# Batch 0's transposed keys are kept in HBM scratch by the first run and loaded back, instead of transposed again

## The chip, the cores and the metric

The kernel runs on one core of a Trainium2 chip. The metric is device time in microseconds (us), the median of three runs. The engines are PE (TensorE, matrix multiply and transpose), DVE (VectorE), ACT (ScalarE), POOL (GpSimd) and SP (SyncE, which here only issues DMAs). Each engine works through its own instructions strictly in the order in which they were written; they meet through semaphores.

## What is computed

Causal attention with a gated linear memory, and behind it a dense mixture of four experts. Cut to what matters:

```python
# q, k, v: (B, H, S, D) = (4, 8, 576, 64)
scores = q @ k.T / sqrt(D), causal mask
a = exp(scores - max); a /= a.sum(-1) + 1e-9
local = a @ v
q_p = phi(q)                                  # elu(q) + 1
mem_out = (q_p @ M_prev) / (q_p @ z_prev + 1e-6)
x = g * mem_out + (1 - g) * local             # g = sigmoid(beta), per head
x = x.transpose(0, 2, 1, 3).reshape(2304, 512)
for e in range(4):                            # w1: (4, 512, 1024), w2: (4, 1024, 512)
    out += p[:, e:e+1] * (relu(x @ w1[e]) @ w2[e])
```

## The kernel before

**Attention.** Heads are taken in pairs, so a tile of 128 partitions holds two heads of 64. The 576 positions are five chunks: four of 128 and a tail of 64. A run is a batch with a set of query chunks: `CA` is chunks 0 and 1, `CB` is chunks 2, 3 and 4. The eight runs go batch 0 to 3 with `CA`, then batch 0 to 3 with `CB`. A task is a run and a head pair.

The very first run, batch 0 with `CA`, is `first_run`. Its order is written out by hand as a string of words, `ORDER`; each word calls the function `f_...` of that name (`ck2` is `f_ck(2)`). It works in plain float32. For head pair `a`, `f_tr` transposes queries and keys on PE, and `f_ck` (a DVE copy) or `f_ka` (an ACT copy) puts the transposed keys of chunks 0 and 1 into the tile `kT[a]`, 128 x 256. The words `d0` to `d10` are matmuls on a tile of zeros whose results nobody reads.

The tiles `qT[a]` and `kT[a]` borrow the buffers of later tiles. For an even `a` they use the tags "ex" and "rl", with one buffer each; for an odd `a` they use two buffers of the tag "qp". So `kT[0]` and `kT[2]` are the same memory, one after the other.

The 28 other tasks are `tasks[0..27]`. Tasks 0 to 11 are `CA` of batches 1 to 3, tasks 12 to 15 are `CB` of batch 0, and tasks 16 to 27 are `CB` of batches 1 to 3. A task loads q, k and v (`t_load`), transposes its key chunks from `t.k0` on into a PSUM tile (`t_trk`), and splits them into a high part rounded to float32r (`k_hi`, two ACT instructions, one per head half) and the rest (`k_lo`, two DVE instructions). `t_cpk` duplicates the high parts over the partition halves by DMA. Tasks 0 to 11 also store the split keys in HBM scratch (`t_keep`), and tasks 16 to 27 take them back (`t_take`), so that they transpose chunks 2 and 3 alone (`t.k0 = 2`). Tasks 12 to 15 transpose all four (`t.k0 = 0`).

**Experts.** The matmuls take each float32 product as three float32r products (high by high, high by low, low by high): `mm1` (L958) and `mm2` (L990) for the phases beside the attention, `pass_parts` (L1189, L1267) for the phases behind it. Weights come by `w_dma` and are split by `w_prep` on ACT and POOL.

**What sets the order.** Attention events carry a slot and a weight (`ev`); the main loop puts attention steps between matmul parts whenever the weight done so far falls behind a target. The weights of `t_trk` count the chunks that it transposes. SP issues nearly all DMAs, each on one of eight completion lanes in turn, and an issue waits until the DMA eight issues before it has landed.

Of the kernel before, what the change touches and what calls it, by code (L numbers as in the profile page):

```python
# [8 lines left out]
F32 = mybir.dt.float32  # L9
# [40 lines left out]
def tile_attention_moe(  # L50
# [13 lines left out]
    nc = tc.nc  # L64
    P = 128
# [9 lines left out]
    CA, CB = (0, 1), (2, 3, 4)  # L75
    NCH = 5
# [25 lines left out]
    GW = 2 * P  # L102
# [8 lines left out]
    dram = ctx.enter_context(tc.tile_pool(name="dram", bufs=1, space=bass.MemoryType.DRAM))  # L111
# [6 lines left out]
    def f(ap):  # L118
        return ap.bitcast(F32)
# [19 lines left out]
    for i in range(2):  # L139
        o, d = i * 12 * P, {}  # L140
# [92 lines left out]
    def batch_load(r):  # L233
        b = r[0]
        zb = att.tile([P, H, D], F32, tag="zb", name=f"zb{b}_{r[1][0]}", bufs=2)
        nc.sync.dma_start(out=zb, in_=z_prev[b : b + 1].partition_broadcast(P)[:, 0])
        bdat[r] = [zb, None, None]

    def batch_load_m(r):
        b = r[0]  # L240
        mr = att.tile([P, H, D], F32, tag="mr", name=f"mr{b}_{r[1][0]}", bufs=1)
        for i in range(2):
            nc.sync.dma_start(
                out=mr[i * D : (i + 1) * D], in_=M_prev[b].rearrange("h d e -> d h e")
            )
        bdat[r][1] = mr
# [16 lines left out]
    for b, cs in RUNS[1:]:  # L263
        for a in range(NPAIR):
            t = Task()
            t.b, t.cs, t.a, t.i, t.s0 = b, cs, a, len(tasks), pos
            t.run = (b, cs)
            t.nk = cs[-1] + 1
            t.k0 = 2 if cs == CB and b else 0
            t.q0 = cs[0] * P  # L270
            t.nq = min((cs[-1] + 1) * P, S) - t.q0
            t.nat, t.qk = NAT[t.i % 2], QK[t.i % 2]
            pos += 4 if cs == CA else 5
            tasks.append(t)
        run_end[t.run] = pos - 1 + 3
# [5 lines left out]

    kept = {}

    def t_load(t, names="qkv"):
        for n, src, c0 in (("q", q, t.cs[0]), ("k", k, t.k0), ("v", v, 0)):
            if n not in names:
                continue
            nfull = min(t.nk, NCH - 1) - c0
            for j in range(2):
                s_ = src[t.b, 2 * t.a + j]  # L290
                nc.sync.dma_start(
                    out=t.nat[n][:, 0:nfull, j],
                    in_=s_[c0 * P : (c0 + nfull) * P].rearrange("(c p) d -> p c d", p=P),
                )
            if t.nk == NCH:
                for r in {"q": (D,), "k": (0,), "v": (0, D)}[n]:
                    to = t.nat["q"][:, 2] if n == "k" else t.nat[n][:, nfull]
                    nc.sync.dma_start(
                        out=to[r : r + S - 4 * P],
                        in_=src[t.b, 2 * t.a : 2 * t.a + 2, 4 * P : S].rearrange(  # L300
                            "h p d -> p h d"
                        ),
                    )
# [53 lines left out]
    def tr(dst, src, n):  # L357
        nc.tensor.transpose(dst, src, ident[0:n, 0:n])  # L358

    def to_tile(name):  # L360
        return ps.tile([P, 512], F32, tag="to", name=name, bufs=2)
# [19 lines left out]
    def k_hi(pt, qk, c0, n):  # L381
        o = slice(c0, c0 + n)
        for x, k_ in ((A, qk["kha"]), (Bh, qk["khb"])):
            nc.scalar.activation(k_[x, o], pt[x, 0:n], AF.Copy)

    def k_lo(pt, qk, c0, n, joint=False):
        o = slice(c0, c0 + n)
        for h, (x, k_) in enumerate(((A, qk["kha"]), (Bh, qk["khb"]))):
            l_ = qk["qz"][x, h * GW : h * GW + n] if joint else qk["kl"][x, o]
            nc.vector.tensor_tensor(l_, pt[x, 0:n], f(k_[x, o]), ALU.subtract)  # L390

    def dup_k(qk, c0, n, eng):
        o = slice(c0, c0 + n)
        for x, y, k_ in ((A, Bh, qk["kha"]), (Bh, A, qk["khb"])):
            eng.dma_start(out=f(k_[y, o]), in_=f(k_[x, o]))

    def copier(t):
        return nc.sync if t.i else nc.scalar

    def flat(ap):  # L400
        return ap.rearrange("p j d -> p (j d)")
# [24 lines left out]
    def t_cpq(t):  # L426
        dup_k(t.qk, 4 * P, D, copier(t))

    def t_trk(t):
        pt = to_tile(f"tk{t.i}")  # L430
        m = min(t.nk, NCH - 1) - t.k0
        for c in range(m):
            tr(pt[:, c * P : (c + 1) * P], flat(t.nat["k"][:, c]), P)
        k_hi(pt, t.qk, t.k0 * P, m * P)
        k_lo(pt, t.qk, t.k0 * P, m * P, t.joint)
        if t.joint:
            t_cpk(t)

    def t_cpk(t):
        dup_k(t.qk, t.k0 * P, (min(t.nk, NCH - 1) - t.k0) * P, copier(t))  # L440

    def t_keep(t):
        kh, kl = (
# [358 lines left out]
    def ev(slot, prio, fn, cost=0.0, vec=0.0):  # L802
        wt = PR["wvec"] + PR["wpe"] * cost + vec
        events.setdefault(slot, []).append((prio, len(events.get(slot, [])), fn, wt))

    def dv(n):
        return 150.0 + n / 0.96

    seen = set()
    for t in tasks:  # L810
        s0 = t.s0
        ld = -9 + t.i if t.i < 2 else s0 - 7
        PQ = PR
        n = len(t.cs)
        if t.run not in seen:
            seen.add(t.run)
            ev(s0 - 9, 9 if t.i else 6, lambda r=t.run: batch_load(r))
            ev(s0 - (5 if t.i else 8), 9, lambda r=t.run: batch_load_m(r))
            ev(s0 + (2 if t.joint else 3), 9 if t.joint else 0.1, lambda r=t.run: batch_prep(r))
            if t.cs == CB and t.b == 0:  # L820
                for i in range(2):
                    ev(s0 - 12, 9, lambda i=i: zeros(i))
        if t.joint:
            ev(ld, 6.3, lambda t=t: t_load(t))
        else:
            ev(s0 - 8, 8, lambda t=t: t_load(t, "qk"))
            ev(s0 - 6, 8, lambda t=t: t_load(t, "v"))
        if t.i:
            p1, p2 = (PQ["phi1"], PQ["phi2"]) if t.i > 1 else ((-4, 6.75), (-4, 7))
            ev(s0 + p1[0], p1[1], lambda t=t: t_phi1(t))  # L830
            ev(s0 + p2[0], p2[1], lambda t=t: t_phi2(t), 0.0, dv(n * P))
        ev(
            s0 + (PQ["phi3"][0] if t.i > 1 else (0, -3)[t.i]),
            PQ["phi3"][1] if t.i > 1 else (6.6, 19)[t.i],
            lambda t=t: t_phi3(t),
            0.0,
            600.0 if t.joint else 750.0,
        )
        ev(s0 - 3 if t.i else s0, 20 if t.i else 6.7, lambda t=t: t_phi4(t))
        if t.i == 0:  # L840
            ev(s0 - 1, 5, lambda t=t: t_trq(t), 109.0 * n, 2 * dv(n * P))
        else:
            ev(s0 + PQ["trq"][0], PQ["trq"][1], lambda t=t: t_trq(t), 109.0 * n, 2 * dv(n * P))
            ev(
                s0 + PQ["trk"][0],
                PQ["trk"][1],
                lambda t=t: t_trk(t),
                109.0 * (t.nk - t.k0),
                2 * dv((4 - t.k0) * P),
            )  # L850
        if not t.joint:
            ev(s0 + PQ["trq"][0] + 1, 0.5, lambda t=t: t_cpq(t))
            ev(s0 + PQ["trk"][0], 2.4, lambda t=t: t_cpk(t))
        if t.joint:
            ev(s0 + 1, 9, lambda t=t: t_keep(t))
        elif t.k0:
            ev(s0 + PQ["trk"][0], 2.3, lambda t=t: t_take(t))
        ev(s0, PQ["v"], lambda t=t: t_v(t))
        ev(
            s0 + PQ["trqp"][0 if t.joint else 2],  # L860
            PQ["trqp"][1],
            lambda t=t: t_trqp(t),
            109.0 * n,
            2 * dv(t.nq),
        )
    for i, s in slots.items():
        w = wid(s.c)
        t = s.t
# [444 lines left out]
    def first_run():  # L1313
        b = FIRST[0]
# [8 lines left out]
        qT, kT, tf, pf, st, ptp, pw, tpf, of = ({} for _ in range(9))  # L1323
# [190 lines left out]
        def f_ldv(c):  # L1514
            for j in range(2):
# [2 lines left out]
                    in_=v[b, j:H:2, c * P : (c + 1) * P].rearrange("a p d -> p a d"),  # L1518
                )

        def f_tq(a):
            tpf[a] = to_tile(f"tpf{a}")
            for c in range(2):
                tr(tpf[a][:, c * P : (c + 1) * P], qp[c][:, a], P)
# [74 lines left out]
        d1 tr0 eb0 d2 cq0 ka0 sc0 sc1 mk00 mk01 tr1 ex00 mk10 d7 ex01 mk11 rc0 d9 ex10  # L1599
        ex11 ck1 rc1 cq1 r1 tr2 np00 ck2 e1 r0 nd11 p1 d0 np01 pt0 np10 sc3 mk30 z1 pa0  # L1600
        mk31 d5 e0 ex31 p0 sc2 mk20 ex30 mk21 tr3 d8 rc3 cq2 rr1 z0 ka3 d10 cq3 ex20 rn1
        ldv1 d6 nm30 nm31 pt1 rr0 ldv0 pa1 sc4 rn0 go9 pt3 mk40 ex21 pa3 mk41 m1 ex40
        rc2 ex41 sc5 nd21 m0 mk50 sc7 np20 tq2 tq0 mk51 eq2 ev0 w0 rc4 pt2 ex50 tq3 sc6
        eq3 mk70 mk71 tq1 ex51 rc5 pa2 ou0 np40 eq1 np41 ex71 pt4 nm51 nd50 mk60 xh0 pt5
        ex60 xl0 ex70 pa5 mk61 pv4 rc7 w1 ou1 ex61 xh1 w2 rc6 xl1 np70 nd71 ou2 nd60
# [25 lines left out]
        for word in ORDER.split():  # L1631
            name = word.rstrip("0123456789")
# [9 lines left out]
        out=mask[:, 4 * P :],  # L1642
        in_=mask[:, 4 * P :],
# [19 lines left out]
    def zeros(i):  # L1663

        nc.gpsimd.memset(f(QK[i]["qb"][:, 2 * P : 3 * P - D]), 0.0)
# [104 lines left out]
```

## Time and profile before

| what | us |
|---|---|
| median of three runs | 977.03 (976.89 to 977.69) |
| the profiled execution: its own time | 976.75 |
| the profiled execution: its span | 974.9 |
| PE busy in the span | 968.4 (99%) |
| DVE, ACT, POOL busy | 664.8, 569.3, 592.3 |

The profile is of one execution. "Busy" is time in which an engine has an instruction in flight. A busy PE need not do useful work: the matmuls on zeros count as well. The chain of waits follows the work that ended last back to its causes, and names at each moment the engine or the DMA that the end depended on. A timeline lists one engine's instructions in order of time; SPq and ACTq are the parts of these engines that issue DMAs.

### The profile page before, as it was taken

The numbers are of one execution on the slowest core, as the hardware profiler recorded it, in microseconds if no ns is written. First come the engines' busy times: TensorE is split into PE (matmuls) and PEld (weight loads), VectorE is DVE, ScalarE is ACT, GpSimd is POOL, SyncE is SP. The second block draws the span as 40 slices with busy tenths as digits, with TensorE's granted clock in tenths as the row PEclk, the third lists the DMA queues.
The fourth block names the chain that finished last, engine by engine and source line by source line (L and its number), as shares of the span: only waits on it lengthen the run. The fifth ranks groups of instructions, "written<-read, shape, count | busy, mean of one in ns | idle before, by whom it ended". The sixth has DMA issues, their size and how long they took to land.

```text
span 974.9 us, 16235 instructions
## 1 busy us (share of the span) xinstructions
PE 968.4 (99%) x5022; PEld 815.7 (84%) x5022; DVE 664.8 (68%) x1787; ACT 569.3 (58%) x1389; POOL 592.3 (61%) x621
## 2 busy tenths in 40 slices
PE   8999999999999999999999999999999999999998
PEld 6889888888888899888888888888888888888887
DVE  6888888988888888888888888834334253342533
ACT  7888866776666788766666675643424233252430
POOL 7999856765665667865568355677255472544620
PEclk9999999999999999999999999999999999999999
DMA  7777565654444267644545332241111111111102
GB/s 176 193 185 220 155 168 147 168 152 110 115 125 119 77 172 197 179 134 107 130 115 139 87 93 66 66 130 55 55 44 55 54 55 53 46 54 46 53 1 87
DMA packets 188263, 106.77 MB, mean 110 GB/s; under 512 B 91664, under 2 KB 168080, under 8 KB 188176
## 3 DMA queue, kind: packets, MB, share of 16 engines
q1 hardware_dynamic: 187600, 105.60, 39.9%
q8 instruction: 40, 0.66, 0.3%
q14 instruction: 47, 0.39, 0.1%
q10 hardware_dynamic: 544, 0.13, 0.1%
q0 software_dynamic: 32, 0.00, 0.0%
HBM read 93.23 MB, written 7.86 MB: 104 GB/s over the span
## 4 chain that ended last, share of the span: by engine, by line
PE 94%; DVE 2%; POOL 1%; DMA 1%; issue 0%; SPq 0%; ACT 0%; DVEq 0%; ACTq 0%
PE y L990 22%; PE h L958 22%; PE y L1267 18%; PE x L1189 9%; PE z L1189 5%; PE pt L358 4%; PE sp L668 4%; PE o L787 4%; PE y L1189 2%; PE o L609 1%; PE tp L358 1%; PE tq L358 1%; PE tk L358 1%; PE sp L523 1%; PE o L781 0%
## 5 line engine op out<-in xcount | busy, mean ns | idle before, releaser
L227 POOL TENSOR_TENSOR w2l<-stg,w2h 128x512 fp32r<-128x512 f32 x128 | 167.4, 1316 | 147.6 <-ACT w2h L224 143.2
L958 PE MATMUL h<-xh,w 128*128 128x512 f32 (+1 forms) x768 | 243.7, 368 | 0.0
L227 POOL TENSOR_TENSOR w<-stg,w 128x512 fp32r<-128x512 f32 x96 | 124.9, 1308 | 139.6 <-ACT w L224 132.5
L958 PEld LDWEIGHTS h<-xh,w 128*128 128x128 f32 x768 | 138.8, 189 | 17.4 <-issue 0.2
L958 PE MATMUL h<-xl,w 128*128 128x512 f32 (+1 forms) x384 | 136.4, 355 | 0.0
L990 PE MATMUL y<-w2h,hh 128*128 128x512 f32 x320 | 134.4, 420 | 0.0
L990 PE MATMUL y<-w2h,hl 128*128 128x512 f32 x320 | 126.2, 394 | 0.2 <-DVE hl L968 0.2
L990 PE MATMUL y<-w2l,hh 128*128 128x512 f32 x320 | 125.8, 393 | 0.3 <-POOL w2l L227 0.3
L1284 DVE SCALAR_TENSOR_TENSOR acc<-y,pn,acc 128x512 f32<-128x512 f32 (+1 forms) x57 | 41.6, 740 | 82.2 <-PE y L1267 82.2
L725 ACT ACTIVATE pt<-pt 128x384 fp32r<-128x384 f32 (+3 forms) x128 | 50.3, 420 | 64.2 <-PE pt L358 63.2
L958 PEld LDWEIGHTS h<-xl,w 128*128 128x128 f32 x384 | 72.8, 190 | 6.1
L990 PEld LDWEIGHTS y<-w2h,hl 128*128 128x128 f32 x320 | 60.1, 188 | 14.4 <-DVE hl L968 1.0
L990 PEld LDWEIGHTS y<-w2l,hh 128*128 128x128 f32 x320 | 60.5, 189 | 7.9 <-POOL w2l L227 1.1
L990 PEld LDWEIGHTS y<-w2h,hh 128*128 128x128 f32 x320 | 60.3, 188 | 7.8
L967 ACT ACTIVATE hh<-h 128x512 fp32r<-128x512 f32 (+1 forms) x96 | 50.4, 525 | 27.4 <-PE h L958 25.7
L727 DVE TENSOR_TENSOR pt<-pt,pt 128x384 fp32r<-128x384 f32 (+3 forms) x128 | 57.4, 468 | 10.7 <-ACT pt L725 9.4
L968 DVE SCALAR_TENSOR_TENSOR hl<-h,hh 128x512 fp32r<-128x512 f32 (+1 forms) x96 | 57.5, 599 | 8.8 <-ACT hh L967 7.7
L358 PE MATMUL pt<-ident,s 128*128 128x128 f32 (+1 forms) x376 | 60.8, 272 | 0.2
L1213 DVE TENSOR_TENSOR cp_a<-y,cp_a 128x512 f32<-128x512 f32 x16 | 11.1, 692 | 71.4 <-PE y L1189 71.4
L358 PEld LDWEIGHTS pt<-ident,s 128*128 128x128 f32 (+1 forms) x376 | 47.0, 139 | 14.2 <-ACT s L721 0.5
L224 ACT ACTIVATE w<-stg 128x512 fp32r<-128x512 f32 x92 | 57.1, 625 | 0.7
L1006 DVE SCALAR_TENSOR_TENSOR acc<-y,pn,acc 128x512 f32<-128x512 f32 x70 | 52.1, 744 | 6.4 <-PE y L990 5.7
(287 smaller groups left out, 2508.8 us busy)
## 6 DMA issues: line engine op xcount, KB each, us to landing
stg<-in_moe_w_dram SPq DMA_DIRECT2D x256, 256.0 KB, 3.0
natall<-in_v_dram SPq DMA_DIRECT2D x32, 128.0 KB, 3.2
natall<-in_q_dram SPq DMA_DIRECT2D x60, 64.0 KB, 3.0
out_dram<-acc SPq DMA_DIRECT2D x15, 256.0 KB, 2.1
natall<-in_k_dram SPq DMA_DIRECT2D x50, 64.0 KB, 2.5
zb<-in_z_prev_dram SPq DMA_DIRECT2D x7, 256.0 KB, 4.5
mr<-in_M_prev_dram SPq DMA_DIRECT2D x14, 128.0 KB, 3.3
natall<-in_v_dram SPq DMA_DIRECT2D x24, 64.0 KB, 2.2
```

Source lines behind the costliest of these rows:

```text
L224: nc.scalar.activation(hi, t, AF.Copy)
L227: nc.gpsimd.tensor_tensor(lo, t, f(hi), ALU.subtract)
L358: nc.tensor.transpose(dst, src, ident[0:n, 0:n])
L725: nc.scalar.activation(dh, src, AF.Copy)
L727: nc.vector.tensor_tensor(dl, src, f(dh), ALU.subtract)
L958: nc.tensor.matmul(pt[0][:, cols], lhsT=w_[:, c], rhs=x_[:, c, cols], start=(c == 0 and z == 0), stop=(c == NKD - 1 and z == 2),)
L967: nc.scalar.activation(h_, pt[0][:, cols], AF.Relu)
L968: nc.vector.scalar_tensor_tensor(l_, pt[0][:, cols], 0.0, f(h_), ALU.max, ALU.subtract)
L990: nc.tensor.matmul(pt[0], lhsT=h_[fc][:, tk], rhs=w_, start=(fc == 0 and z == 0), stop=(fc == HF - 1 and z == 2),)
L1006: nc.vector.scalar_tensor_tensor(acc[g, tt], pt[0], pe, acc[g, tt], ALU.mult, ALU.add)
L1189: nc.tensor.matmul(k_, lhsT=w_[:, c], rhs=x_[:, c], start=new and n == 0, stop=n == 5, skip_group_check=True,)
L1267: nc.tensor.matmul(y0, lhsT=a[:, tk], rhs=w_[:, x0:x1], start=(fc == 0 and z == 0), stop=(fc == HF - 1 and z == 2),)
```

## The change

`first_run` gets a new word `kp`: `kp0` to `kp3` each issue one DMA from SP that stores `kT[a]` in HBM scratch (`kf`). The first three stand just ahead of the loads of v (`ldv1`), the fourth after `go9`. Tasks 12 to 15 now have `k0 = 2`. They load chunks 2 and 3 naturally and the stored keys of chunks 0 and 1, already transposed, into the free half of their key tile (`raw_k`); they transpose two chunks instead of four, and split the loaded part in four further instructions (two of ACT, two of DVE) that read it from SBUF.

```diff
-            t.k0 = 2 if cs == CB and b else 0
+            t.k0 = 2 if cs == CB else 0
...
+    def raw_k(t):
+        return t.nat["k"][:, 2:4].rearrange("p c j d -> p (c j d)")
...
+            if n == "k" and t.nk == NCH and not t.b:
+                nc.sync.dma_start(out=raw_k(t), in_=kept[t.a])
...
         k_hi(pt, t.qk, t.k0 * P, m * P)
         k_lo(pt, t.qk, t.k0 * P, m * P, t.joint)
+        if t.cs == CB and not t.b:
+            k_hi(raw_k(t), t.qk, 0, GW)
+            k_lo(raw_k(t), t.qk, 0, GW)
...
     def t_cpk(t):
-        dup_k(t.qk, t.k0 * P, (min(t.nk, NCH - 1) - t.k0) * P, copier(t))
+        c0 = t.k0 if t.b else 0
+        dup_k(t.qk, c0 * P, (min(t.nk, NCH - 1) - c0) * P, copier(t))
...
-        elif t.k0:
+        elif t.b:
             ev(s0 + PQ["trk"][0], 2.3, lambda t=t: t_take(t))
...
+        def f_kp(a):
+            kept[a] = dram.tile([P, GW], F32, tag=f"kf{a}", name=f"kf{a}")
+            nc.sync.dma_start(out=kept[a], in_=kT[a])
...
         mk31 d5 e0 ex31 p0 sc2 mk20 ex30 mk21 tr3 d8 rc3 cq2 rr1 z0 ka3 d10 cq3 ex20 rn1
-        ldv1 d6 nm30 nm31 pt1 rr0 ldv0 pa1 sc4 rn0 go9 pt3 mk40 ex21 pa3 mk41 m1 ex40
+        kp0 kp1 kp2 ldv1 d6 nm30 nm31 pt1 rr0 ldv0 pa1 sc4 rn0 go9 kp3 pt3 mk40 ex21 pa3 mk41 m1 ex40
```

Both programs, as built, show where the new instructions stand. First SP in the first run, before. `pn` are expert probabilities, `xr` here holds batch 0's v, and a name such as DMAHW5 is a completion lane.

```order
L1625 DMA xr_100<-in_M_prev_dram 64x4x64 [waits DMAHW2_49]
L925 DMA pn_76<-in_moe_domain_probs_dram 128x4x4 [waits DMAHW3_49]
L925 DMA pn_76<-in_moe_domain_probs_dram 128x4x4 [waits DMAHW4_49]
L1516 DMA xr_100<-in_v_dram 128x4x64 [waits DMAHW5_49,DVE_49]
L1516 DMA xr_100<-in_v_dram 128x4x64 [waits DMAHW6_49]
```

The same place now; `kf0` is the scratch, `tw0_1` is `kT[0]`, `tw1_1` is `kT[1]` and `tw2_1` is `kT[2]`.

```order
L1638 DMA xr_100<-in_M_prev_dram 64x4x64 [waits DMAHW2_49]
L934 DMA pn_76<-in_moe_domain_probs_dram 128x4x4 [waits DMAHW3_49]
L934 DMA pn_76<-in_moe_domain_probs_dram 128x4x4 [waits DMAHW4_49]
L1532 DMA kf0_320<-tw0_1_191 128x256 [waits DMAHW5_49,Activation_49]
L1532 DMA kf1_322<-tw1_1_220 128x256 [waits DMAHW6_49,DVE_49]
L1532 DMA kf2_324<-tw2_1_251 128x256 [waits DMAHW7_49,DVE_49]
L1525 DMA xr_100<-in_v_dram 128x4x64 [waits DMAHW0_49,DVE_49]
```

Three stores stand between the loads of `pn` and of v, and the first of them is the third DMA on lane 5.

Next DVE, around the word `ck2`, which copies the keys of head pair 2 (`tg2`, PSUM) into `kT[2]`. Before:

```order
L1422 RECIPROCAL stf1_223<-stf1_223 128x2 [waits DVE_49]
L1356 COPY tw2_1_251<-tg2_245 128x256 [waits PE_49]
L1438 TENSOR_SCALAR sf1_222,dump_78<-sf1_222,stf1_223 128x256 [waits DVE_49]
L1492 SCALAR_TENSOR_TENSOR xr_100<-natall_79,ep1_254 128x4x128 [waits DMAHW3_49,DMAHW6_49,DMAHW2_49,Activation_49]
L1388 ISA sf3_271,stf3_272<-pf3_0_267,mask_70 128x256 [waits PE_49]
```

Now:

```order
L1431 RECIPROCAL stf1_223<-stf1_223 128x2 [waits DVE_49]
L1365 COPY tw2_1_251<-tg2_245 128x256 [waits DMAHW5_49,PE_49]
L1447 TENSOR_SCALAR sf1_222,dump_78<-sf1_222,stf1_223 128x256 [waits DVE_49]
L1501 SCALAR_TENSOR_TENSOR xr_100<-natall_79,ep1_254 128x4x128 [waits DMAHW3_49,DMAHW6_49,DMAHW2_49,Activation_49]
L1397 ISA sf3_271,stf3_272<-pf3_0_267,mask_70 128x256 [waits PE_49]
```

Nothing moved, but the copy into `kT[2]` has a new wait, on lane 5. In the built program it asks for the lane's third landing, which is that of `kf0`.

Last PE, at the key transposes of task 13 (`tk`); `h` and `y` are expert matmuls. Before:

```order
L958 MATMUL h_3_3060<-xl,w_111 128x512
L958 MATMUL h_3_3060<-xh,w_111 128x512
L358 MATMUL tk_3090<-ident,natall 128x128 x4
L958 MATMUL h_3_3060<-xh,w_111 128x512
L958 MATMUL h_3_3060<-xl,w_111 128x512
```

Now:

```order
L967 MATMUL h_3_3066<-xl,w_111 128x512
L967 MATMUL h_3_3066<-xh,w_111 128x512
L363 MATMUL tk_3107<-ident,natall 128x128 x2
L999 MATMUL y_1_0_3118<-w2h_112,hh_103 128x512
L999 MATMUL y_1_0_3118<-w2l_113,hh_103 128x512
```

Four transposes became two, and the step stands three matmuls later: the smaller weights in `ev` shift the attention steps by a few matmuls against the expert work, here and all through the phases beside the attention.

## Rows read from the trace of the kernel before

**Rows 1.** Page, busy time of each engine, and the granted clock in slices.

```profile
PE 968.4 (99%) x5022; PEld 815.7 (84%) x5022; DVE 664.8 (68%) x1787; ACT 569.3 (58%) x1389; POOL 592.3 (61%) x621
...
PEclk9999999999999999999999999999999999999999
```

**Rows 2.** Stretches: length, busy us of PE, PEld, DVE, ACT, POOL; clock, DMA.

```profile
0.00:25.00 25.00, 22.53 (x139) 15.84 (x140) 17.65 (x86) 18.68 (x61) 17.77 (x34) 1.00 0.77 176
...
50.00:75.00 25.00, 25.00 (x166) 22.30 (x167) 21.13 (x69) 19.82 (x55) 23.04 (x22) 1.00 0.77 197
...
175.00:200.00 25.00, 25.00 (x138) 21.06 (x137) 23.15 (x74) 18.84 (x55) 19.72 (x22) 1.00 0.69 180
```

**Rows 3.** Chain of waits, first 62 us: start, length, what (xcount merged).

```profile
5.40 4.32 DMA natall<-in_k_dram
...
9.76 0.33 PE tg L358
...
13.86 0.70 DVE rp L1501
...
17.56 0.60 POOL w L226
...
30.49 3.42 DMA stg<-in_moe_w_dram
...
48.57 1.29 POOL w2l L227
...
49.90 0.73 PE y L990 x2
...
57.61 0.22 PE tk L358 x2
```

**Rows 4.** Timeline of SP's DMA issues: start, length, line, target, xcount.

```profile
11.56 1.15 SPq L925 DMA_DIRECT2D pn<-in_moe_domain_probs_dram  x2
14.58 2.02 SPq L1516 DMA_DIRECT2D xr<-in_v_dram  x4
...
25.23 0.98 SPq L291 DMA_DIRECT2D natall<-in_v_dram  x2
26.85 1.39 SPq L243 DMA_DIRECT2D mr<-in_M_prev_dram  x2
```

**Rows 5.** Timeline of DVE at the copy into kT[2]; brackets: idle before, releaser.

```profile
10.13 0.43 DVE L1356 COPY tw<-tg 128x256 f32<-128x256 f32 x1 [0.93 <-PE tg L358]
10.47 0.47 DVE L1438 TENSOR_SCALAR_CACHE_REDUCE sf<-sf,stf 128x256 f32<-128x256 f32 x1
```

**Rows 6.** DMA issues by target: xcount, KB each, median us from issue to landing.

```profile
xr<-in_v_dram SPq DMA_DIRECT2D x4, 128.0 KB, 3.0
...
out_dram<-acc SPq DMA_DIRECT2D x6, 128.0 KB, 2.3
```

**Rows 7.** The two pn loads (L925): time to landing.

```profile
DMA to landing us min/median/max: 3.2/3.5/3.7
```

**Rows 8.** Timeline of PE in the first run: matmuls on zeros (L1596), a wait.

```profile
1.45 2.08 PE L1596 MATMUL ids<-hh 128*128 128x512 f32 x4 [1.45 <-DVE hh L1636]
3.33 1.06 PE L1596 MATMUL id<-hh 128*128 128x512 f32 x2
...
9.76 0.33 PE L358 MATMUL tg<-ident,natall 128*128 128x128 f32 x1 [0.90 <-DMA natall<-in_k_dram]
...
13.02 1.65 PE L1596 MATMUL id<-hh 128*128 128x512 f32 x6
```

**Rows 9.** Instructions on tk: ns min/median/max, first and last start, shapes.

```profile
L384 ACT ACTIVATE kha<-tk x28: 360/368/592, 26.1 to 569.5; 64x256 fp32r<-64x256 f32 x24, 64x512 fp32r<-64x512 f32 x4
...
L390 DVE TENSOR_TENSOR kl<-tk,kha x16: 406/417/682, 186.9 to 570.3; 64x256 fp32r<-64x256 f32 x12, 64x512 fp32r<-64x512 f32 x4
```

**Rows 10.** ACT instruction of the same shape reading SBUF: busy us, mean ns.

```profile
L416 ACT ACTIVATE qz<-qa 64x256 fp32r<-64x256 f32 x5 | 2.1, 418 | 0.1
```

## The prediction

> **What bounds the kernel now.** I read the busy times first: PE is busy 99% of the span and no other engine over 68% [rows 1]. The windows say where the missing part lies: PE is short of full in the first 25 us, and full to the last digit in the stretches behind [rows 2]. But PE's first 25 us are padded with matmuls on zeros, so a busy PE there proves nothing, and I went on to the chain of waits. It has two regimes. From 49.90 us on it is PE (expert matmuls and transposes) practically to the end; what leaves PE's stream there is worth its full length, and what other engines do is free while PE stays fed [rows 2, 3]. Before that the chain does not run through PE's capacity. It goes from a key load (5.40 us, 4.32 long) to the PE transpose of the keys of head pair 2 at 9.76, from there to DVE (13.86), to POOL's weight splits (17.56), to a weight load (30.49), to POOL again (48.57) and then to PE [rows 3]. So the kernel is a serial start of 50 us and then a full PE, and whatever delays the start delays everything.
>
> **The change, part by part.** I sum against the profiled execution, 976.75 us (its span is 974.9, so 1.85 lies around it); the median of the three runs is 0.28 above it, and I add that at the end.
>
> *Transposes removed.* Tasks 12 to 15 drop two each, eight in all. In the chain two key transposes take 0.22 us [rows 3], so 0.11 each: 8 x 0.11 = 0.88 us off PE, in a stretch in which PE is full. This is the whole gain.
>
> *The split of the loaded keys.* Per task, ACT had two instructions over 64x512 (592 ns as the row's longest); now it has two over 64x256 from PSUM (368 each) and two from SBUF, for which the nearest row is 418 ns [rows 9, 10]: 2 x (368 + 418 - 592) = 0.39 us more. DVE goes from 2 x 682 to four; the SBUF ones have no row of their own shape, and I take the PSUM row's 417 for each of the four [rows 9]: 4 x 417 - 1364 = 0.30 us more. Both are off the path: in this stretch DVE is busy 23.15 of 25 us and ACT 18.84 while PE waits for nothing [rows 2]. If DVE's 1.85 us of slack were gone, the four tasks would cost at most 4 x 0.30 = 1.2 us on DVE. I count 0 and keep 1.2 as the bound above.
>
> *Loads.* Each of the four tasks issues one more DMA on SP and loads the same bytes. SP is not on the chain there: 0. The new instruction that duplicates the keys waits on SP for the second pair of ACT instructions, under 1 us later than before, with weight loads queued behind it that are buffered six deep: 0.
>
> *Pacing.* The smaller weights move attention steps by a few matmuls against expert work. The work on PE is the same; a step that lands too early could make PE wait, one that lands later could spare a wait. PE shows no idle time to spare behind 50 us [rows 2], so there is nothing to gain, and I bound the loss by two or three matmul times, 0.5 us; count 0.
>
> *The stores, on SP.* SP finishes issuing the `pn` loads at 11.56 + 1.15 = 12.71 and then stands until 14.58, when it issues the loads of v [rows 4]. The three stores fall into that gap of 1.87 us at some 0.5 us each, so as issue time they cost nothing. The fourth stands behind them; its 0.5 us is covered by the pause between 25.23 + 0.98 = 26.21 and 26.85 [rows 4], and if that cover were gone it would cost 0.5.
>
> *The new wait, on DVE.* This is the term that decides. `kT[2]` lies in the memory of `kT[0]`, so the DVE copy `ck2` may not start before the store `kf0` has read `kT[0]` and landed; the built program has that wait. Before, `ck2` ran at 10.13, straight after PE had delivered the transpose, and DVE went on without a pause [rows 5]. But `kf0` stands on SP behind the `pn` loads, so it is not even issued before 12.71 plus the usual 0.05 between issues, 12.76. From issue to landing a store of 128 KB takes 2.3 us (median of six, on quiet queues) [rows 6]; the loads of `pn`, issued just ahead into a full queue, took 3.2 to 3.7 [rows 7]; the 128 KB loads of v, issued just behind, 3.0 [rows 6]. I take 3.0, the nearest in place and size, and keep 2.3 and 3.7 as bounds. `kf0` lands at 15.76 (15.06 to 16.46), DVE resumes 0.04 later as PE did behind its load (5.40 + 4.32 = 9.72, start at 9.76) [rows 3], at 15.80. The stall is 15.80 - 10.13 = 5.67 us (4.97 to 6.37).
>
> [...]
>
> *Who waits behind it.* DVE is in order: behind `ck2` stand a normalisation, the phi of the queries, the masks of head pair 1 and the reduction at 13.86 that the chain goes through [rows 3, 5]. ACT waits for the phi and the masks, POOL for the same, PE for the PSUM bank that `ck2` empties; SP waits for `ck2` itself before `kf2`, and then for the reduction before the loads of v, with all later loads behind. `kf1` has landed long before ACT reaches its one wait on it. Between 10.13 and 13.86 DVE's row of work is gapless, and from 13.86 the chain hands over engine by engine to 49.90. I see no link that waited for something the stall doesn't delay, so all 5.67 us pass to the end.
>
> *The sum.* +5.67 - 0.88 = +4.79. 976.75 + 4.79 = 981.54, and with 0.28 for the median 981.8 us. With the bounds of the landing 981.1 to 982.5.
>
> **The rivals.**
>
> [...]
> [...]
>
> *The stall is swallowed.* The other side: the chain between 17.56 and 49.90 runs over POOL and a weight load of 3.42 us [rows 3]; if the weight splits there were held by loads that SP issued early rather than by POOL's late start, the start would catch up. The first four weight tiles are indeed issued ahead of the stall. If all of it is swallowed, only the gain stays: 977.03 - 0.88 = 976.1. From the stall, 2.8 us must be swallowed before the result is no longer slower. Against it: POOL's first split at 17.56 comes behind work that depends on DVE's reduction, and every load behind v waits on SP for DVE too.
>
> *The wait is not for the store.* If DVE's wait were for an older DMA on lane 5, long landed, DVE would not stall, `kf0` would find whatever is in the memory, and the time would be 976.1 as well. The wait's count, the lane's third landing, speaks against it.
>
> **How the numbers follow.** Forecast (stall passes whole, clock holds) 0.54; clock falls and costs 0.28; swallowed wholly or mostly 0.11; wait not for the store 0.03; pacing or the longer splits cost over 1 us beyond the forecast 0.04. The likeliest gives 981.8. The range must leave out at most 0.2: it begins at 980.2, the lower bound of 981.1 less about 1 us for a stall partly swallowed, and ends at 984.0, the upper bound 982.5 plus the 1.5 of the clock. It leaves out the two cases near 976 and half of the last. About 0.2% is what a measurement of this kernel can tell from no change, so faster means below 975.1 and slower above 979.0. No case gives faster but an error in all of this, 0.02; within 0.2% are the swallowed stall and the wrong wait, together 0.13; slower is the rest, 0.85.
>
> **What would show it.** In the profile after, DVE's copy into `kT[2]` should start at 15.1 to 16.5 instead of 10.13, idle before it, with the DMA of `kf` as its releaser; the chain should go through SP's issues and that DMA at 12.8; the first PE stretch of the chain should begin near 55.5 instead of 49.90; POOL's first split near 23 instead of 17.56; eight `tk` transposes fewer, and PE full behind 56. [...] I am wrong if the copy starts before 14, or if it starts late but the chain reaches its PE regime less than 3 us later than before.

## The result, and the profile after

| | median, us | lowest to highest | ratio to before, 95% interval |
|---|---|---|---|
| before (beside it) | 976.96 | 975.88 to 978.58 (6 runs) | |
| after | 983.75 | 983.23 to 984.22 (6 runs) | 1.0072 [1.0061, 1.0082] |

The change makes the kernel 6.8 us slower. The forecast was +4.8 (981.8 us); the time lies inside the range, close to its upper end. The profiled execution of after took 983.94 us with a span of 982.1, 7.2 more than before.

First the page of after: the busy time of PE and the granted clock in 40 slices. The rows of before are [rows 1].

```profile
PE 970.3 (99%) x5014; PEld 816.2 (83%) x5014; DVE 662.8 (67%) x1795; ACT 570.5 (58%) x1397; POOL 591.3 (60%) x621
...
PEclk7999999999999999999999999999999999999999
```

Eight matmuls fewer [rows 1], as the diff says, and yet 1.9 us more busy time on PE. The clock digit says where to look: in the first slice (24.6 us) the clock was not full, as it was all through before. Up to the start of the full PE (57.50 here, 49.90 before) PE is busy 49.22 us instead of 46.88, so the surplus lies in the start.

Next the chain of waits of after (start, length, what), to be read against [rows 3].

```profile
12.67 2.81 DMA kf<-tw
15.57 0.44 DVE tw L1365
16.05 1.22 PE id L1609 x2
...
19.05 2.67 PE id L1609 x6
...
56.17 1.29 POOL w2l L227
57.50 0.73 PE y L999 x2
```

Three things differ. The chain now goes through the landing of the first store and the DVE copy that waited for it; behind the copy it goes on through PE, where before it went through DVE and POOL; and its second regime, the full PE, begins at 57.50 instead of 49.90. So 7.60 us are lost in the start. From there to a mark late in the program (the first row of 21 second-layer matmuls that the chain merges) it takes 617.00 - 49.90 = 567.10 us before and 624.26 - 57.50 = 566.76 after: 0.34 us are won back. What remains is the span's 7.2, but for rounding. Here the mark in the chain of before and of after, and the same two stretches as windows (length, busy us of PE, PEld, DVE, ACT, POOL; clock, DMA):

```profile
617.00 4.78 PE y L990 x21
```

```profile
624.26 4.78 PE y L999 x21
```

```profile
49.90:617.00 567.10, 566.99 (x3145) 485.89 (x3146) 478.11 (x1426) 401.79 (x1040) 375.52 (x391) 1.00 0.51 137
```

```profile
57.50:624.26 566.76, 566.50 (x3137) 484.88 (x3138) 475.91 (x1433) 403.07 (x1048) 375.05 (x391) 1.00 0.51 137
```

The wait itself, on the timeline of DVE in after (brackets: idle before, releaser), and SP's issues, against [rows 5] and [rows 4]:

```profile
15.57 0.42 DVE L1365 COPY tw<-tg 128x256 f32<-128x256 f32 x1 [6.57 <-DMA kf<-tw]
```

```profile
11.42 1.15 SPq L934 DMA_DIRECT2D pn<-in_moe_domain_probs_dram  x2
12.67 3.67 SPq L1532 DMA_DIRECT2D kf<-tw  x3
20.18 2.04 SPq L1525 DMA_DIRECT2D xr<-in_v_dram  x4
```

The copy starts at 15.57 instead of 10.13, 5.44 us late. That leaves 7.60 - 5.44 = 2.16 us of the start. They are PE's: here PE's timeline behind the copy, and stretches of 1 us (length, busy us of PE, PEld, DVE, ACT and POOL, granted clock, share and rate of DMA).

```profile
16.05 1.22 PE L1609 MATMUL id<-hh 128*128 128x512 f32 x2 [5.95 <-DVE tw L1365]
...
18.82 2.90 PE L1609 MATMUL id<-hh 128*128 128x512 f32 x6
```

```profile
11.00:12.00 1.00, 0.00 (x0) 0.00 (x0) 0.00 (x0) 0.00 (x0) 0.00 (x0) 1.00 1.18 319
12.00:13.00 1.00, 0.00 (x0) 0.00 (x0) 0.00 (x0) 0.00 (x0) 0.00 (x0) 0.50 1.21 263
...
21.00:22.00 1.00, 1.00 (x5) 0.70 (x4) 0.56 (x3) 0.00 (x0) 1.00 (x2) 0.50 0.60 138
22.00:23.00 1.00, 1.00 (x9) 0.65 (x8) 0.07 (x1) 0.49 (x1) 0.81 (x1) 0.88 0.87 197
```

PE stood for 5.95 us; 1.9 us into that, at 12, the granted clock fell to half (0.50), and it came back only in the stretch from 22 to 23. The six matmuls on zeros that took 1.65 us before [rows 8] took 2.90. From 16.05 to 48.89 nearly all of the chain lies on PE.

### The profile page after: what moved, and what is told of

It reads as the page before. It is cut to its first block, busy times and chain, and to the rows that moved or that the text cites. A ratio compares the mean times of both kernels' runs of the same rounds, so it can differ in the third digit from the quotient of the medians.

```text
span 982.1 us, 16253 instructions
## 1 busy us (share of the span) xinstructions
PE 970.3 (99%) x5014; PEld 816.2 (83%) x5014; DVE 662.8 (67%) x1795; ACT 570.5 (58%) x1397; POOL 591.3 (60%) x621
## 4 chain that ended last, share of the span: by engine, by line
PE 96%; DVE 1%; SPq 1%; DMA 1%; POOL 0%; issue 0%; ACT 0%; DVEq 0%
PE y L999 22%; PE h L967 22%; PE y L1276 18%; PE x L1198 9%; PE z L1198 4%; PE pt L363 4%; PE sp L677 4%; PE o L796 4%; PE y L1198 2%; PE o L618 1%; PE tq L363 1%; PE tp L363 1%; PE tk L363 1%; PE sp L532 1%; PE o L790 0%; POOL w2l L227 0%
```

## The experiments

The theory after this reading: the memory of the key buffers is the cause; the wait for the store costs 5.4 us because it lands late, and passes whole; the clock's fall adds some 2 us; the eight transposes give back a few tenths. What could be otherwise: that the new loads, splits or weights cost something in the long stretch; that the clock's fall is without effect; and, on the store, why it lands so late (its place in SP's row, its engine, or what is on its way ahead of it). In the table the ratios are against runs of before on the same chip (their medians were 976.46 to 976.96), "copy" is the start of the DVE copy, "regime" the chain's first piece of two second-layer matmuls, "stretch" from there to the same mark as above; "PE stood" is the pause that the copy ended. The times are medians of all executions; the columns behind the interval tell of the one that was profiled.

| kernel | median, us | ratio to before, 95% interval | copy | PE stood | clock | regime | stretch |
|---|---|---|---|---|---|---|---|
| before | 976.96 | | 10.13 | | full | 49.90 | 567.10 |
| after | 983.75 | 1.0072 [1.0061, 1.0082] | 15.57 | 5.95 | half 12 to 22 | 57.50 | 566.76 |
| e1_own_memory | 976.19 | 0.9995 [0.9987, 1.0004] | 9.30 | | full | 49.17 | 566.86 |
| e2_pe_kept_busy | 982.22 | 1.0057 [1.0044, 1.0070] | 16.08 | 0.50 | full | 55.88 | 566.75 |
| e3_stores_only | 984.17 | 1.0076 [1.0063, 1.0088] | 15.43 | 5.35 | half 13 to 20 | 56.43 | 566.85 |
| e4_own_memory_old_weights | 976.03 | 0.9990 [0.9980, 0.9999] | 9.52 | | full | 49.78 | 566.53 |
| e5_store_earlier | 984.11 | 1.0077 [1.0064, 1.0091] | 15.15 | 5.42 | half 12 to 22 | 58.05 | 566.70 |
| e6_store_from_act | 983.15 | 1.0066 [1.0052, 1.0080] | 14.22 | 3.04 | half 13 to 19 | 56.18 | 566.74 |
| e8_no_split | 976.05 | 0.9996 [0.9987, 1.0005] | 9.78 | | full | 49.66 | 567.12 |
| e9_new_weights_only | 976.69 | 0.9999 [0.9990, 1.0008] | 9.57 | | full | 50.33 | 567.30 |
| e10_weights_behind_store | 978.88 | 1.0024 [1.0015, 1.0033] | 11.12 | | full | 52.19 | 566.83 |
| e11_half_behind_store | 981.78 | 1.0050 [1.0033, 1.0067] | 12.81 | 1.83 | half 12 to 18 | 54.85 | 566.77 |
| e12_sync_store_first | 977.90 | 1.0014 [1.0004, 1.0023] | 10.70 | 0.94 | full | 51.30 | 566.68 |
| e13_both_stores_first | 976.36 | 0.9999 [0.9990, 1.0008] | 10.22 | 0.53 | full | 49.98 | 566.68 |

**e1: the first two key buffers in memory of their own.** Everything of the change stays; `kT[0]` and `kT[1]` are put into a part of `natall` that is free in the first run, so no later buffer lies on them.

```diff
+                if n and a < 2:
+                    o = (17, 21)[a] * P
+                    d[a] = natall[:, o : o + GW]
+                    continue
```

> The change as it is, but the stored keys of head pairs 0 and 1 lie in memory of their own (a part of the load buffer that nothing else uses then), so that no copy has to wait for a store. Theory A (the new wait of DVE for the first store, and the clock that fell behind it, are the whole loss): DVE's copy into kT[2] starts near 10 us again, the granted clock is 1.00 all through, the chain reaches PE's regime near 50 us, and the time is 976.1 to 976.6 us. Rival B (the stores and loads cost time themselves, as traffic or on SP's queue): the copy starts near 10 us, but the time stays above 979 us.

The loss is gone. DVE's copy is back behind PE, with no DMA to wait for (timeline of DVE in e1), and the regime starts at 49.17 (chain of e1):

```profile
9.30 0.42 DVE L1369 COPY tw<-tg 128x256 f32<-128x256 f32 x1 [0.42 <-PE tg L363]
```

```profile
49.17 0.73 PE y L999 x2
```

All four stores, loads and splits are still there. So the whole loss is the wait on the memory, and what hangs on it.

**e2: PE kept busy in the pause.** In the changed kernel, one of the words that place matmuls on zeros, `d0`, places 26 instead of 2. On PE they stand just ahead of where it stood idle, and they do not need the copy.

```diff
-            for _ in range(2):
+            for _ in range(26 if j == 0 else 2):
```

> The change as it is, with 24 more matmuls on zeros on PE just ahead of where it stood idle. DVE's wait stays. Theory A (5.4 us of the loss are DVE's stall, some 2.2 us are PE's clock at half behind its idle time): the copy still starts near 15.5 us, the granted clock stays at 1.00, the chain reaches PE's regime at 55.3 instead of 57.5 us, and the time is 981.5 us (981.2 to 981.9). Rival C (the 2.2 us come from SP's later loads or from the order, not from the clock): the time stays at 983.7 us with the clock at 1.00.

Timeline of PE in e2 at the pause, and a stretch of 1 us in it:

```profile
9.05 6.16 PE L1609 MATMUL id<-hh 128*128 128x512 f32 x26
...
16.56 0.70 PE L1379 MATMUL pf<-tw,tw 64*128 64x256 f32 x2 [0.50 <-DVE tw L1365]
```

```profile
15.00:16.00 1.00, 1.00 (x5) 0.43 (x3) 0.00 (x0) 0.53 (x2) 0.00 (x0) 1.00 0.43 140
```

The copy is even later than in after (16.08, +5.95 over before), but the clock stays full and the regime starts at 55.88, +5.98: now the stall passes one to one, and the 2.16 us are gone. They were the clock's. The time agrees: e2's median is 1.53 us below that of after although its copy is 0.51 later, 2.04 together; that later copy is also why 982.22 lies above the 981.2 to 981.9 that were expected. One caution: a matmul behind the filler ends just when the store lands, so the trace names PE as the copy's releaser. But in `ORDER` that matmul (`sc3`) comes behind the copy (`ck2`), so the copy cannot wait for it; the store landed at 15.99, and the copy started 0.09 us later, as in after (15.48 and 15.57).

**e3: the stores alone.** The kernel before with the four stores added; nothing loads them.

```diff
+        def f_kp(a):
+            kept[a] = dram.tile([P, GW], F32, tag=f"kf{a}", name=f"kf{a}")
+            nc.sync.dma_start(out=kept[a], in_=kT[a])
...
-        ldv1 d6 nm30 nm31 pt1 rr0 ldv0 pa1 sc4 rn0 go9 pt3 mk40 ex21 pa3 mk41 m1 ex40
+        kp0 kp1 kp2 ldv1 d6 nm30 nm31 pt1 rr0 ldv0 pa1 sc4 rn0 go9 kp3 pt3 mk40 ex21 pa3 mk41 m1 ex40
```

> The kernel before with the four stores in the first run alone; nobody reads them, and tasks 12 to 15 transpose four chunks as before. Theory A: stall and slow clock as in the changed kernel, nothing given back: 976.96 + 7.6 = 984.5 us. Rival D (part of the loss lies in tasks 12 to 15, in the loads or the longer splits): clearly less than 984, 977 to 982 us.

Timeline of DVE in e3:

```profile
15.43 0.43 DVE L1356 COPY tw<-tg 128x256 f32<-128x256 f32 x1 [5.96 <-DMA kf<-tw]
```

The stores bring the same wait and the same loss by themselves. Whether e3 is slower than after by what the transposes give cannot be said: the two intervals overlap.

**e4: e1 with the planner's old weights.** The two lines in which the change made the attention steps cheaper for the planner are put back.

```diff
-                109.0 * (t.nk - t.k0),
-                2 * dv((4 - t.k0) * P),
+                109.0 * (t.nk - (t.k0 if t.b else 0)),
+                2 * dv((4 - (t.k0 if t.b else 0)) * P),
```

> As the run with own memory, but the planner's weights of the four tasks count four chunks as before, so that PE's order is that of the kernel before with eight transposes fewer. From the first PE piece of the chain to the first stretch of 96 y matmuls the kernel before takes 613.29 us and the changed one 612.88, 0.41 less where eight transposes at 0.11 are 0.88. If the shifted order ate the rest: 612.4 here, and 612.9 in the run with own memory. If the longer splits on ACT and DVE ate it: 612.9 in both. The total would be 976.1 or 976.6 us.

At 0.9990 [0.9980, 0.9999] its ratio is the lowest of all, and the only one whose interval lies below no change, if barely; it overlaps that of e1. A gain of 0.88 us would be 0.0009 of the time, which is about what these intervals can resolve. The weights decide nothing that the time can show here.

**e5: the store issued earlier on SP.** The first store goes ahead of the loads of `M_prev` and the probabilities, right behind the weight tiles.

```diff
+        def f_mp(i):
...
-        d1 tr0 eb0 d2 cq0 ka0 sc0 sc1
+        d1 tr0 eb0 d2 cq0 ka0 kp0 mp0 sc0 sc1
```

> The change with the first store moved up on SP, ahead of the loads of M_prev and of pn, so that it is issued near 9 us instead of 12.7. Theory E (a store lands only behind all that SP queued ahead of it, and the four weight tiles issued from 6.5 to 9 us landed at 11.8 to 14.7): it lands near 14.8, the copy starts at 14.8 to 15.0, the clock falls again, and the time is 982.5 to 983.5 us. Rival F (the store takes its own 3 us from issue): it lands near 12.2, the stall is 2.1 us, PE's pause is too short to slow the clock, and the time is 978.3 to 979 us.

Issue and landing in the chain of e5, and the copy on DVE's timeline:

```profile
8.71 6.35 DMA kf<-tw
```

```profile
15.15 0.42 DVE L1365 COPY tw<-tg 128x256 f32<-128x256 f32 x1 [6.04 <-DMA kf<-tw]
```

Issued 3.96 us earlier than in after (8.71 against 12.67), the store lands 0.42 us earlier (15.06 against 15.48). The hour of issue is not what sets the landing. The copy and the time came out above the ranges that were given for this case (15.0 and 983.5 us): behind the copy the start lost another 3.13 us here, 2.16 in after.

**e6: the first two stores issued by ACT.** In another queue than SP's loads, and earlier: `kp0` stands behind `ka0` and `kp1` behind `cq1`.

```diff
-            nc.sync.dma_start(out=kept[a], in_=kT[a])
+            (nc.sync if a > 1 else nc.scalar).dma_start(out=kept[a], in_=kT[a])
```

> The change with the first two stores issued by ACT, right behind the copy that writes kT[0] (near 6 us) and behind the one of qT[1] (near 9 us); the other two stay on SP. If ACT's queue goes beside SP's: the first store lands by 9 to 10 us, the copy starts near 10 us as before, the clock stays, and the time is 976.2 to 977.2 us (two issues of 0.5 us on ACT, the second perhaps on the path). If a store of ACT's queue also waits for what SP queued: it lands at 12 to 14, the stall is 2 to 4 us, and the time 978.5 to 981 us.

Chain of e6, and its issues around 8 us (target, KB, median us to landing):

```profile
7.95 6.19 DMA kf<-tw
```

```profile
stg<-in_moe_w_dram SPq DMA_DIRECT2D x2, 256.0 KB, 6.6
kf<-tw ACTq DMA_DIRECT2D x1, 128.0 KB, 6.2
```

The store lands at 14.14 though ACT had queued nothing else near it, in the midst of the landings of the four weight loads that SP had issued around it: the third, issued at 7.52, landed at 13.74, and the fourth, issued at 8.07, at 15.04. Against after, an issue 4.72 us earlier (7.95 against 12.67) brought a landing 1.34 us earlier (14.14 against 15.48). So the idea that it stands behind others in SP's queue falls, and the time, 983.15, lies above both ranges that were expected. The idea that was left is that what is on its way ahead of it, on whichever queue, must land first: z_prev and three of the weight tiles, 1 MB (the expectation of e10 counts the fourth too). e10 and e11 vary that.

**e8 and e9: what the rest of the change costs.** e8 is e4 without the four instructions per task that split the loaded keys (the score matmuls still run, on what stands in the splits' targets, one of which two more memsets fill with zeros); e9 is the kernel before with the planner's new weights alone.

```diff
-        if t.cs == CB and not t.b:
-            k_hi(raw_k(t), t.qk, 0, GW)
-            k_lo(raw_k(t), t.qk, 0, GW)
```

> The run with own memory and old weights, but tasks 12 to 15 leave out the split of the loaded keys (so batch 0's scores of chunks 2 to 4 against chunks 0 and 1 use stale keys); two more memsets of POOL early in the first run. It asks who took part of the 0.88 us. If the longer splits on ACT and DVE did: the stretch from the chain's first PE piece to its 21 y matmuls near 617 us is 566.0 us instead of 566.5. If not, it stays at 566.5, and the time at 976.0 us.

> The kernel before with the planner's new weights alone: no store, no load, all transposes. The attention steps stand where they stand in the changed kernel. If the shifted order costs PE something: the same stretch is 567.4 to 567.7 us instead of 566.9 to 567.1 in the two runs with the old order, with a wait of PE for a split weight near 390 us, and the time is 977.1 to 977.4 us. If not: 566.9 to 567.1, and 976.8 us.

Both times are no change within their intervals, and e8's median is e4's to 0.02 us. So neither the splits nor the weights have a cost that the time can show. The stretches settle less: e8's, 567.12, was expected at 566.0 or 566.5 and is longer than e4's 566.53, half of it by one wait of 0.30 us of PE for DVE at 69.05 that e4 does not have; e9's is 0.20 longer than that of before.

**e10 and e11: the weight tiles behind the store.** e10 is after with ACT issuing the first store and all four 256 KB weight loads moved behind `M_prev` and the probabilities; e11 moves two of the four.

```diff
-        for _ in range(NSTG):
-            w_dma()
         m4 = M_prev[b].rearrange("(a j) d e -> j d a e", j=2)
...
         c_probs((b, 1 - b))
+        for _ in range(NSTG):
+            w_dma()
```

> The changed kernel, with ScalarE issuing the first store (as in the run e6_store_from_act, where it was issued at 7.95 and landed at 14.14) and the four 256 KB loads of weight tiles moved behind M_prev and the two loads of probabilities. Theory Q (the store lands only when the bytes queued ahead of it, on whichever queue, have landed; in e6 those are 1.25 MB): only z_prev's 256 KB and the last query and key loads are ahead now, so it lands at 10.2 to 11.0, the DVE copy starts by 11.1, TensorE idles under 1.6 us and keeps its clock, and the time is 975.8 to 978.0. Theory S (a store issued this early takes 6 us of itself): the copy starts at 14.2 as in e6 and the time is 982.5 to 984.2.

> The same with only two of the four loads of weight tiles moved behind: 768 KB lie ahead of the store. Theory Q: the landing lies about half way, the copy starts at 12.0 to 12.8, and the time is 978.0 to 979.6, or 979.5 to 981.8 if TensorE's clock falls as well. Theory S: copy at 14.2, 982.5 to 984.2.

The first store in e10 (issues around 8 us; it was issued at 7.86) and in e11 (chain):

```profile
kf<-tw ACTq DMA_DIRECT2D x1, 128.0 KB, 3.2
```

```profile
7.80 4.92 DMA kf<-tw
```

Issued within 0.15 us of each other, the store takes 3.2, 4.9 and 6.2 us with none (e10), two (e11) and three (e6) of the weight loads ahead. The first two, 512 KB, cost 1.7 us. That is about the rate at which the core's DMA engines were moving bytes anyway (285 and 338 GB/s in the 1-us stretches from 10 to 12 in e6, so 1.6 to 1.8 us for 512 KB). The step to e6, 1.3 us, is more than one load of 256 KB at that rate; the fourth load, issued 0.12 us behind the store, may have taken part. So in these runs the store landed behind the bytes that were already on their way.

In time, e11 came where its second figure said (979.5 to 981.8, with the clock's fall). e10 missed: 978.88 against at most 978.0. Its copy was on time (11.12, +0.99), but the regime came 2.29 us late. The timeline of ACT in e10 shows a second wait of the same kind:

```profile
16.37 0.39 ACT L1359 ACTIVATE tw<-tf 128x256 f32<-128x256 f32 x1 [1.48 <-DMA kf<-tw]
```

This is `cq3`, the copy of head pair 3's queries into `qT[3]`, which lies on `kT[1]`. So ACT waits for the second store; that one stood on SP, issued at 12.05 behind the weight loads, and took 4.30 us.

**e12 and e13: stores ahead of the weight tiles, all on SP.** e12 issues the first store ahead of the four weight loads, e13 both of the first two.

```diff
-        d1 tr0 eb0 d2 cq0 ka0 sc0 sc1 mk00 mk01 tr1 ex00 mk10 d7 ex01 mk11 rc0 d9 ex10
-        ex11 ck1 rc1 cq1 r1 tr2
+        d1 tr0 eb0 d2 cq0 ka0 kp0 mp0 sc0 sc1 mk00 mk01 tr1 ex00 mk10 d7 ex01 mk11 rc0 d9 ex10
+        ex11 ck1 rc1 cq1 kp1 wt0 r1 tr2
```

(This is e13's; `mp0` issues `M_prev` and the probabilities, `wt0` the weight tiles. In e12 `wt0` stands behind `kp0` and includes `mp0`, and `kp1` stays where it was.)

> The changed kernel with all stores still on SyncE, but the first one issued ahead of the four loads of weight tiles, which stand behind it with M_prev and the probabilities. SyncE then waits for the first key pair's write (about 7.9 in the run e5_store_earlier, whose store was issued at 8.71 behind the weight tiles and landed at 15.06). Theory Q: issue at about 8.0, landing at 10.3 to 11.2, copy by 11.3, time 975.8 to 978.2; the weight tiles land 2 us later, and their first reader on GpSimd, at 24.47 in the changed kernel, waits for none of them. Theory S: copy at 14 to 15, 982.5 to 984.2.

> As e12_sync_store_first, but the second store too is issued ahead of the four loads of weight tiles (behind the first one, M_prev and the probabilities); e12 left ScalarE waiting 1.06 us for the second store, which was issued at 12.46 and landed at 15.51. Theory Q (a store lands behind the bytes queued ahead of it): the second store is issued by 9.5 and lands by 12, ScalarE no longer waits for it, the first store lands at 9.6 to 10.6 with z_prev and M_prev ahead or beside it, the copy on VectorE starts by 10.7, the chain reaches its piece of two second-layer matmuls at 50.0 to 50.8 (49.90 before, 51.30 in e12), and the time is 976.0 to 977.3, which is the time before within its uncertainty: all of the loss is the stores' landing. If weight tiles that land 3 us later hold up GpSimd instead, the piece lies at 51 or later and the time is 977.5 to 979.

The copy in e12 and, below, in e13 (timelines of DVE), and the regime in the chain of e13:

```profile
10.70 0.42 DVE L1365 COPY tw<-tg 128x256 f32<-128x256 f32 x1 [1.55 <-DMA kf<-tw]
```

```profile
10.22 0.42 DVE L1365 COPY tw<-tg 128x256 f32<-128x256 f32 x1 [1.14 <-PE pf L1379]
```

```profile
49.98 0.73 PE y L999 x2
```

e12 came out as expected (977.90, copy at 10.70). What it still loses, 1.40 us at the regime, is for the larger part ACT's wait of 1.06 us in `cq3` for the second store, which was issued at 12.46 and landed at 15.51; the chain goes through it.

With e13 the time is that of before, without more on-chip memory, and ACT waits for no store. DVE still does, though the trace names PE: the transposes that the copy reads were done by 8.86, and the matmul that is named comes behind the copy in `ORDER`, as in e2. Here are these transposes on PE's timeline, the first store on SP's, and its time to landing:

```profile
8.48 0.38 PE L363 MATMUL tg<-ident,natall 128*128 128x128 f32 x2
```

```profile
6.58 0.35 SPq L1532 DMA_DIRECT2D kf<-tw  x1
```

```profile
kf<-tw SPq DMA_DIRECT2D x1, 128.0 KB, 3.6
```

The store landed at 10.13, and the copy started 0.09 us behind it. Against the profiled execution of before this wait of 1.14 us costs nothing, since there the copy had to wait for a late key load and started at 10.13 too [rows 5, 8]. Against e1, whose copy waits for no store, the regime comes 0.81 later; the medians, 976.19 and 976.36, cannot be told apart.

The weight tiles, issued from 10.23 instead of 6.49, are late for nobody: POOL's first split stands at 17.61 (17.56 before [rows 3]). But e13 is not faster than before: even with the loss gone the change brings nothing that can be measured.

## Why the prediction was right, and where it was not

**The deciding term was right in place and mechanism, and close in size.** The copy into `kT[2]` waits for the store `kf0`; it starts at 15.57 (forecast 15.80, bounds 15.10 to 16.50), the stall is 5.44 us (5.67), the landing took 2.81 us (3.0, bounds 2.3 and 3.7). e1 shows that the buffer's memory is the cause, e3 that the stores alone suffice. The start that it is counted from is that of one execution: without a store the copy starts at 9.30 to 9.78 in e1, e4, e8 and e9, so counted from there the stall would be up to 6.3 us.

**The reason given for the landing was only half of it.** The step started from the hour of issue and read the delay as the store's place behind the `pn` loads on SP. e5 and e6 show that issuing it 4 to 4.7 us earlier would have moved the landing by 0.4 to 1.3 us. What the landing followed is the weight loads on their way: 3.2 us after issue with none of them ahead (e10), 4.9 with two (e11), 6.2 with three (e6). At 12.67 two of the four weight loads had landed (at 11.62 and 12.52), two had not (13.56 and 14.50); the second `pn` load followed at 15.29 and the store at 15.48. That the time of a load of v in another place, 3.0 us, fitted what was left of this row was in part luck.

**The stall passes whole: right.** In e2, where the clock holds, +5.95 at the copy gives +5.98 at the regime. Nothing was swallowed, so that rival falls, and so does the one by which the wait was not for the store: DVE's releaser in after is that DMA.

**The clock was the step that the likeliest case had wrong.** That the clock holds was the likeliest case; its fall stood at 0.28, and the upper end of the range takes in 1.5 us for it. No run shows these 1.5 us. What the runs show in their place: the granted clock fell to 0.50 in after, e3, e5, e6 and e11, and in after that cost 2.16 us in the profile (7.60 - 5.44). Before, PE is not on the chain between 13.86 and 48.57 [rows 3]; the chain of after goes through PE there from 16.05 on. In after the clock stayed at half for 10 us, 4 of them while PE stood. Over the kernels in which the clock fell, the regime came later by 1.2 (e3), 2.2 (after and e6), 2.3 (e11) and 3.1 us (e5) more than the copy; where it held and only the first store was waited for (e2, e13) by 0.0. The smallest of these figures says little by itself: in e9, with the full clock and no store, the same sum gives 1.0, since the chain there runs through PE and not through the copy. With the cost that after shows, the likeliest case would have read 981.8 plus 2.2, 984.0; the median was 983.75. That the time lies inside the range at all is owed to the 1.5 us, which the upper end had taken in.

**The gain was a term that was mis-sized.** In the chain, from the regime to the late mark, `tk` pieces take 6.35 us before (58 of them) and 5.45 after (50): the eight transposes give their 0.9. But the stretch is only 0.34 shorter. Over the kernels the same holds: those with the loads stand at 566.53 to 566.86 in it (but e8 at 567.12), those without at 566.85 to 567.30. Of the other half microsecond, 0.15 is time in which PE stands: 0.11 us of the stretch before (567.10 - 566.99), 0.26 in after (566.76 - 566.50), 0.25 in e1, and 0.11 again in e4, which has the old weights. That points to the pacing, which was taken at nothing, but these are single executions. Where the rest goes is not settled.

**The splits, the loads and SP's issue time at nothing: right**, as far as e1, e8 and e13 can tell.

Of the signs named ahead, the DMA in the chain at 12.67 and the releaser were there; POOL's first split came at 24.47 instead of near 23 and the regime at 57.50 instead of near 55.5, both by the clock's 2 us.

## What to carry to other kernels

Before a store is added to a buffer that is reused, look who writes the buffer next and what is on its way to or from memory by then: here the writer waited for the landing (5.44 us in after), and the landing came later with more bytes of loads ahead of it, though another engine had queued them (3.2 us after issue with no weight load ahead in e10, 6.2 with three in e6). What mended it here was to issue the small store ahead of the bulk loads (e13, where 1.14 us of waiting were left and cost nothing that the time shows), or to give the buffer memory of its own (e1); to issue it from another engine did not (e6, 983.15 us). And when a stall leaves PE without work for some microseconds, look at the granted clock too: where it fell here, the regime came 1.2 to 3.1 us later on top of stalls of 2.7 to 5.4, and filler that bridged the pause gave 2.16 us back (e2).

## What the runs showed of the hardware that was not expected

A store in ACT's queue landed behind loads in SP's queue: 6.2 us after issue with 768 KB of weight loads ahead (e6), 4.9 with 512 KB (e11), 3.2 with none (e10). In e11 it also began late: issued at 7.80, it had moved no packet by 10; 24 packets of ACT's queue moved from 10 to 11 and 113 from 11 to 12. In e6, issued at 7.95, it had moved none by 9.6; in e10, issued at 7.86, none by 8.8 and 95 from there to 9.6.

The granted clock fell in e11 though PE stood for only 1.83 us; the 1-us stretches of e11 before and at the fall:

```profile
10.00:11.00 1.00, 0.82 (x3) 0.51 (x4) 0.38 (x2) 0.97 (x4) 0.77 (x3) 1.00 1.13 336
11.00:12.00 1.00, 0.46 (x2) 0.06 (x1) 0.00 (x0) 1.00 (x3) 0.16 (x1) 0.76 1.13 283
```

It fell as the pause began, behind 3 us in which PE had been busy 0.63 to 0.82 of the time. In after it held for nearly 2 us of the pause, behind stretches in which PE was full; in e6, where PE had been busy 0.73 and 0.68 in the stretches from 9 to 11, it held for 1 us of the pause. In e12, where PE was full until a pause of 0.94, it held in the profiled execution; but in one of e12's ten executions (980.57 us) and one of e10's (980.24) the mean granted clock was 0.996, and in one of before, beside e1 (981.26), 0.997. What decides is not shown. Once fallen, the clock stayed at half for 6 us (e3, e6, e11) to 10 us (after), counted in whole stretches of 1 us, and PE was mostly busy again in them.
